# Polysketch attention and hash routing: attention written as a fixed pipeline over batches, with products of ones ahead of it and gather lists of the static slots alone

## The chip, the cores and the metric

The kernel runs on one core of one Trainium2 chip. The metric is the device time of one launch in microseconds (us); before the change it is 277.99 us, the median of three runs (277.56, 277.99 and 279.6). The engines are named as in the profile: PE (TensorE's matmuls) and PEld (its weight loads), DVE (VectorE), ACT (ScalarE), POOL (GpSimd), SP (SyncE, which here only issues DMAs).

## The reference

Attention with a polynomial feature map over 4 batches, 4 heads, 1088 positions and a head width of 32, then a mixture of 8 experts in which a token's id picks its expert:

```python
def phi(x):                                    # S1, S2: (8, 32), float64 in memory
    a = einsum('rd,bhsd->bhsr', S1, x); b = einsum('rd,bhsd->bhsr', S2, x)
    return einsum('bhsi,bhsj->bhsij', a, b).reshape(..., 64)
q_p, k_p = phi(q), phi(k)
num = q_p @ (k_p^T v);  den = q_p @ sum_s(k_p) + 1e-06
x = (num / den) as rows (4352, 128)            # one row per batch and position, heads side by side
e = token_ids * 2654435761 % 8
out[e == i] = relu(x[e == i] @ w1[i]) @ w2[i]  # w1: (8, 128, 1024), w2: (8, 1024, 128), float32
```

## The kernel before, in words

**Attention.** Of each batch's 1088 positions, 1024 are its main part (8 tiles of 128 positions) and 64 its tail. For the keys, `k_side` (lines 302 to 324) transposes two groups of 4 tiles on PE (`kT`, L309), copies them with ACT (L311), multiplies by the sketches (`ab`, L313), copies that with ACT (L316) and makes the 64 features on DVE (`kp`, L328). `kv_side` (lines 331 to 352) then sums the features times the values, with a column of ones for the denominator, over all tiles (`kv`, L340); ACT spreads the result over the matrix `m` in 16 copies (L349). `q_side` (lines 354 to 400) makes the features of the queries in two halves: blocks transposed on DVE (`qT`, L358), sketches on PE (`abq`, L365), features (`f`, L328) and transposes (`fT`, L378) on DVE. It multiplies them by `m` (`x`, L387), ACT copies (`xe`, L391), DVE inverts the denominators (`den`, L393 and L394), POOL divides (`xs`, L397), and ACT issues the store of the rows to the scratch tensor `x_rows` in HBM (L404). Written k0, q1 and so on below: the part with the number of the batch, from 0.

**The tails** of all four batches are features of one tile pair. Their keys are done first; their queries are done once, after batch 3's `kv` (line 412), from copies of `m` (`m_tail`, L351), and stored by four small DMAs (L415) ahead of batch 3's main rows.

**Routing.** Each expert has 2 x 288 static slots: the first 288 are filled from batches 0 to 2 alone, the others from all. A count by scans and three products (`cnt`, L191), then some forty small DVE operations (lines 188 to 258) give each token its slot. Lines 266 to 282 turn slots into lists: per 17 token columns, DVE compares (`row`, L270; `in_tile`, L273; two `til`, L277), and 34 PE products add up the token numbers (`idx_ps`, L280). The lists `get` and `put` have 68 columns: 36 tiles of static slots and 32 for tokens beyond them.

**Experts.** For 16 groups of 288 slots, POOL gathers rows by indirect DMA (`xg`, L424), PE transposes (`xp`, L464), multiplies by `w1` and `w2` (`hp`, L488; `op`, L496), transposes back (L475), and POOL scatters (L429). The first 18 tiles' gathers read only rows of batches 0 to 2. The loop behind it (line 517) serves tokens beyond the static slots; with these inputs no expert has more than 566 tokens, so it makes no turn.

**What sets the order.** Nothing is placed by hand: the framework's scheduler orders each engine's instructions, and DMAs wait for their buffers. Loads go out on SP (q, k, v, weights) and ACT (token ids and the 12 tail pieces, L88).

Of the kernel before, what the change touches and what calls it, by code (L numbers as in the profile page):

```python
# [9 lines left out]
F32 = mybir.dt.float32  # L10
# [14 lines left out]
def kernel(  # L25
# [12 lines left out]
    nc = tc.nc  # L38
# [38 lines left out]

    s64 = const.tile([2 * R, D, 2], I32)
# [29 lines left out]

    ident = const.tile([P, P], F32)
    make_identity(nc, ident[:])  # L110
    iota = const.tile([P, P], F32)
    nc.gpsimd.iota(iota[:], pattern=[[1, P]], base=0, channel_multiplier=0, allow_small_or_imprecise_dtypes=True)
    nval = const.tile([P, C], I32)
    nc.gpsimd.iota(nval[:], pattern=[[1, C]], base=1, channel_multiplier=C)
# [24 lines left out]
    ex = shifts("ex", hi, 1, 21)  # L139
    live = s_tile("live", F32)  # L140
    nc.vector.tensor_scalar(ex[:], ex[:], 127.0 - 1023.0, 0.0, op0=OP.add, op1=OP.max)
    nc.vector.tensor_scalar(ex[:], ex[:], 255.0, None, op0=OP.min)
    nc.vector.tensor_scalar(live[:], ex[:], 0.0, None, op0=OP.is_gt)
    nc.vector.tensor_scalar(ex[:], ex[:], 23, None, op0=OP.logical_shift_left)
    sg = s_tile("sg")
    nc.vector.tensor_scalar(sg[:], hi, 31, 31, op0=OP.logical_shift_right, op1=OP.logical_shift_left)
    nc.vector.tensor_tensor(sg[:], sg[:], ex[:], op=OP.bitwise_or)
    m_hi = shifts("m_hi", hi, 12, 9)
    m_lo = s_tile("m_lo")
    nc.vector.tensor_scalar(m_lo[:], lo, 29, None, op0=OP.logical_shift_right)  # L150
    top = s_tile("top")
    nc.vector.tensor_tensor(top[:], m_hi[:], m_lo[:], op=OP.bitwise_or)
    nc.vector.tensor_tensor(top[:], top[:], sg[:], op=OP.bitwise_or)
    rest = shifts("rest", lo, 3, 3)
    s32 = s_tile("s32", F32)
    nc.vector.tensor_copy(s32[:], rest[:])
    nc.vector.scalar_tensor_tensor(s32[:], s32[:], 2.0 ** -52, sg[:].bitcast(F32), op0=OP.mult, op1=OP.mult)
# [9 lines left out]
    s_k = const.tile([P, Q, 2, R], F32)  # L167
    nc.gpsimd.memset(s_k[:], 0.0)
    for t in range(Q):
# [7 lines left out]
    eid_i = const.tile([P, C], I32)  # L177
    nc.vector.tensor_scalar(eid_i[:], tok[:, :, 0], E - 1, None, op0=OP.bitwise_and)
    eid = const.tile([P, C], F32)
    nc.vector.tensor_copy(eid[:], eid_i[:])  # L180
    mask = hots.tile([P, E, C], F32)
    nc.vector.tensor_tensor(mask[:], eid[:].unsqueeze(1).to_broadcast([P, E, C]),
                            iota[:, 0:E].unsqueeze(2).to_broadcast([P, E, C]), op=OP.is_equal)
    seq = hots.tile([P, E, C], F32)
    nc.vector.tensor_tensor_scan(seq[:].rearrange("p e c -> p (e c)"), keep[:].rearrange("p e c -> p (e c)"),
                                 mask[:].rearrange("p e c -> p (e c)"), 0.0, op0=OP.mult, op1=OP.add)
    cp = const.tile([P, E], F32)
    nc.vector.tensor_copy(cp[:], seq[:, :, C - 1])
    cnt = bank([P, 3, E], "cnt")
    for n, w in enumerate((before, ones, early)):  # L190
        nc.tensor.matmul(cnt[:, n], w[:], cp[:], start=True, stop=True)  # L191
    first = const.tile([P, E], F32)
    nc.vector.tensor_copy(first[:], cnt[:, 0])

    took = const.tile([P, E], F32)
    nc.vector.tensor_scalar(took[:], cnt[:, 2], float(GN), None, op0=OP.min)
    nt_f = const.tile([P, E], F32)
    nc.vector.tensor_tensor(nt_f[:], cnt[:, 1], took[:], op=OP.subtract)
    nc.vector.tensor_scalar(nt_f[:], nt_f[:], float(P - 1 - GN), 0.0, op0=OP.add, op1=OP.max)
# [11 lines left out]
    past = hots.tile([P, OT, E], F32)  # L211
# [10 lines left out]
    def of_token(per_expert, name):  # L222

        both = hots.tile([P, E, C], F32, name=name + "_m")
        nc.vector.tensor_tensor(both[:], mask[:], per_expert[:].unsqueeze(2).to_broadcast([P, E, C]), op=OP.mult)
        t = const.tile([P, C], F32, name=name)
        nc.vector.tensor_reduce(t[:], both[:].rearrange("p e c -> p c e"), axis=AX.X, op=OP.add)
        return t

    nc.vector.tensor_tensor(seq[:], seq[:], first[:].unsqueeze(2).to_broadcast([P, E, C]), op=OP.add)  # L230
    nc.vector.tensor_mul(seq[:], seq[:], mask[:])
    rank = const.tile([P, C], F32)
    nc.vector.tensor_reduce(rank[:], seq[:].rearrange("p e c -> p c e"), axis=AX.X, op=OP.add)
    took_t = of_token(took, "took_t")
    jump_e = const.tile([P, E], F32)
    nc.vector.tensor_sub(jump_e[:], ends[:], nt[:])
    nc.vector.tensor_scalar(jump_e[:], jump_e[:], float(P), float((E - 1) * GN), op0=OP.mult, op1=OP.add)
    nc.vector.scalar_tensor_tensor(jump_e[:], iota[:, 0:E], float(-GN), jump_e[:], op0=OP.mult, op1=OP.add)
    jump = of_token(jump_e, "jump")
    pos = const.tile([P, C], F32)  # L240
    nc.vector.tensor_sub(pos[:], rank[:], took_t[:])
    nc.vector.scalar_tensor_tensor(jump[:], pos[:], float(GN), jump[:], op0=OP.is_gt, op1=OP.mult)

    late = const.tile([P, C], F32)
    nc.vector.memset(late[:], 1.0)
    nc.vector.tensor_scalar(late[0:EP], rank[0:EP], float(GN), None, op0=OP.is_gt)
    nc.vector.tensor_scalar(took_t[:], took_t[:], -1.0, float(E * GN), op0=OP.mult, op1=OP.add)
    nc.vector.tensor_add(took_t[:], took_t[:], jump[:])
    nc.vector.tensor_mul(took_t[:], took_t[:], late[:])
    nc.vector.tensor_add(rank[:], rank[:], took_t[:])  # L250
    nc.vector.scalar_tensor_tensor(rank[:], eid[:], float(GN), rank[:], op0=OP.mult, op1=OP.add)
    slot_i = const.tile([P, C], I32)
    nc.vector.tensor_scalar(slot_i[:], rank[:], -1.0, None, op0=OP.add)
    st_i = const.tile([P, 2, C], I32)
    nc.vector.tensor_scalar(st_i[:, 0], slot_i[:], P.bit_length() - 1, None, op0=OP.logical_shift_right)
    nc.vector.tensor_scalar(st_i[:, 1], slot_i[:], P - 1, None, op0=OP.bitwise_and)
    st = const.tile([P, 2, C], F32)
    nc.vector.tensor_copy(st[:], st_i[:])


    digit_i = const.tile([P, 2, C], I32)
    nc.vector.tensor_scalar(digit_i[:, 0], nval[:], 6, None, op0=OP.logical_shift_right)
    nc.vector.tensor_scalar(digit_i[:, 1], nval[:], 63, None, op0=OP.bitwise_and)
    digit = const.tile([P, 2, C], F32)
    nc.vector.tensor_copy(digit[:], digit_i[:])
    idx_ps = ps_x.tile([P, 2, NT], F32, tag="x", name="idx_ps")
    CH = C // 2
    for c0 in range(0, C, CH):
# [30 lines left out]
    for m in ms + m_tails:  # L299
        nc.gpsimd.memset(m[:], 0.0)  # L300
# [275 lines left out]
```

## Time and profile before

| | us |
|---|---|
| median of the runs shown | 277.99 |
| the profiled execution | 277.01 |
| its span, first to last instruction | 275.3 |
| PE busy in it | 224.0 |
| DVE busy | 103.5 |
| POOL busy | 96.0 |
| ACT busy | 69.8 |

The profile is of one execution, and 1.7 us of its time lie outside the span. The span has two halves: attention and routing, to about 118 us, in which engines wait for one another, and the experts, in which PE is busy almost without a gap. PE's records are modelled at their ends, so a run of like products is best read as its length divided by its count. The granted clock is a column of its own; 1.00 is 2.4 GHz and 0.50 is 1.2 GHz.

### The profile page before, as it was taken

The numbers are of one execution on the slowest core, as the hardware profiler recorded it, in microseconds if no ns is written. First come the engines' busy times: TensorE is split into PE (matmuls) and PEld (weight loads), VectorE is DVE, ScalarE is ACT, GpSimd is POOL, SyncE is SP. The second block draws the span as 40 slices with busy tenths as digits, with TensorE's granted clock in tenths as the row PEclk, the third lists the DMA queues.
The fourth block names the chain that finished last, engine by engine and source line by source line (L and its number), as shares of the span: only waits on it lengthen the run. The fifth ranks groups of instructions, "written<-read, shape, count | busy, mean of one in ns | idle before, by whom it ended". The sixth has DMA issues, their size and how long they took to land.

```text
span 275.3 us, 3183 instructions
## 1 busy us (share of the span) xinstructions
PE 224.0 (81%) x1109; PEld 188.0 (68%) x1110; DVE 103.5 (38%) x200; ACT 69.8 (25%) x197; POOL 96.0 (35%) x114
## 2 busy tenths in 40 slices
PE   0079898879896986427999999999999999999900
PEld 0069898869796986405777777777777777777600
DVE  6682992099614693001213213213223213222100
ACT  0121306112543233201322222332322332322200
POOL 7200003001640041277705565265562522421340
PEclk9999999988795695955999999999999999999975
DMA  5994344998110001031100111011110100000000
GB/s 164 275 340 124 87 144 120 337 343 268 78 79 0 0 2 76 19 114 49 48 12 24 43 38 41 30 36 35 47 39 19 45 21 18 17 18 15 19 26 8
DMA packets 22464, 22.14 MB, mean 80 GB/s; under 512 B 5178, under 2 KB 19771, under 8 KB 22448
## 3 DMA queue, kind: packets, MB, share of 16 engines
q1 hardware_dynamic: 15840, 14.69, 17.7%
q0 software_dynamic: 2304, 4.59, 5.8%
q10 hardware_dynamic: 4304, 2.66, 3.1%
q8 instruction: 9, 0.15, 0.2%
q14 instruction: 7, 0.06, 0.1%
HBM read 17.47 MB, written 4.59 MB: 80 GB/s over the span
## 4 chain that ended last, share of the span: by engine, by line
PE 59%; DMA 14%; issue 11%; ACT 6%; POOL 4%; DVE 3%; POOLq 1%; ACTq 0%; SPq 0%; DVEq 0%
PE hp L488 17%; PE op L496 14%; DMA out_dram<-os,put 9%; PE x_ps L387 7%; PE kv L340 6%; PE ab_ps L313 6%; ACT m L349 4%; PE abq_ps L365 3%; PE kT_ps L309 2%; POOL out_dram L429 2%; DMA k<-in_k_dram 2%; DMA q<-in_q_dram 2%; PE idx_ps L280 1%; ACT kT L311 1%; PE xp L464 1%
## 5 line engine op out<-in xcount | busy, mean ns | idle before, releaser
L488 PE MATMUL hp<-xT,w 128*128 128x288 f32 x256 | 84.8, 419 | 0.0
L496 PE MATMUL op<-hT,w 128*128 128x288 f32 x256 | 81.9, 406 | 0.0
L439 DVE TENSOR_SCALAR hT<-hp 128x288 f32<-128x288 f32 x64 | 29.3, 458 | 88.9 <-PE hp L488 88.9
L496 PEld LDWEIGHTS op<-hT,w 128*128 128x128 f32 x256 | 48.6, 190 | 13.3
L429 POOL DMA_INDIRECT out_dram<-os,put x36 | 35.8, 993 | 61.3 <-ACT os L437 30.4
L488 PEld LDWEIGHTS hp<-xT,w 128*128 128x128 f32 x256 | 48.3, 197 | 11.5
L437 ACT ACTIVATE hT<-hp 128x288 f32<-128x288 f32 x64 | 26.3, 411 | 67.1 <-PE hp L488 66.0
L424 POOL DMA_INDIRECT xg<-x_rows,get x36 | 36.5, 1015 | 17.4 <-PE xp L464 9.0
L387 PE MATMUL x_ps<-m,fT 128*128 128x132 f32 x128 | 24.4, 360 | 2.0 <-ACT m L349 1.4
L387 PEld LDWEIGHTS x_ps<-m,fT 128*128 128x128 f32 x128 | 22.5, 265 | 3.0 <-ACT m L349 2.1
L313 PE MATMUL ab_ps<-s_k,kT 128*128 128x64 f32 (+1 forms) x72 | 17.9, 422 | 6.1 <-ACT kT L311 6.1
L313 PEld LDWEIGHTS ab_ps<-s_k,kT 128*128 128x128 f32 (+1 forms) x72 | 16.3, 328 | 8.6 <-ACT kT L311 7.1
L397 POOL TENSOR_TENSOR xs<-xe,den 128x512 f32<-128x512 f32 (+1 forms) x9 | 11.5, 1296 | 30.4 <-DVE den L394 25.3
L319 POOL MEMSET va<- 128x32 f32 x4 | 0.6, 155 | 51.3 <-PE kv L340 51.3
L340 PE MATMUL kv<-va,kp 128*128 128x66 f32 x128 | 18.5, 309 | 0.0
L340 PEld LDWEIGHTS kv<-va,kp 128*128 128x128 f32 x128 | 18.2, 227 | 0.0
L349 ACT COPY m<-kv 32x66 f32<-32x66 f32 x64 | 13.2, 206 | 19.1 <-PE kv L340 18.2
L464 PE MATMUL xp<-ident,xg 128*128 128x128 f32 x36 | 7.6, 303 | 10.8 <-DMA xg<-x_rows,get 10.8
L464 PEld LDWEIGHTS xp<-ident,xg 128*128 128x128 f32 x36 | 5.0, 148 | 14.2 <-issue 8.0
L391 ACT COPY xe<-x_ps 128x396 f32<-128x396 f32 (+2 forms) x17 | 6.2, 380 | 26.8 <-PE x_ps L387 24.6
L365 PE MATMUL abq_ps<-s_k,qT 128*128 128x64 f32 (+1 forms) x72 | 12.7, 346 | 0.0
L365 PEld LDWEIGHTS abq_ps<-s_k,qT 128*128 128x128 f32 (+1 forms) x72 | 12.2, 262 | 0.4 <-issue 0.3
(129 smaller groups left out, 167.2 us busy)
## 6 DMA issues: line engine op xcount, KB each, us to landing
w<-in_moe_w_dram SPq DMA_DIRECT2D x16, 512.0 KB, 7.8
k<-in_k_dram SPq DMA_DIRECT2D x4, 512.0 KB, 4.6
v<-in_v_dram SPq DMA_DIRECT2D x4, 512.0 KB, 5.4
q<-in_q_dram SPq DMA_DIRECT2D x4, 512.0 KB, 5.2
x_rows<-xs ACTq DMA_DIRECT2D x4, 512.0 KB, 2.6
xg<-x_rows,get POOLq DMA_INDIRECT x36, 2.6
out_dram<-os,put POOLq DMA_INDIRECT x36, 2.3
k_tail<-in_k_dram ACTq DMA_DIRECT2D x4, 32.0 KB, 5.0
```

The costliest lines, as they stand in the source:

```text
L313: nc.tensor.matmul(ab_ps[:, g:g + w, h].rearrange("p t x r -> p t (x r)"), kT[:w * D, h], s_k[:w * D, 0:w].rearrange("p t x r -> p (t x r) ...
L340: nc.tensor.matmul(kv[:, pr], kp[rows, t, 2 * pr:2 * pr + 2].rearrange("p h i j -> p (h i j)"), va[rows, t, 2 * pr:2 * pr + 2].rearrange(" ...
L349: nc.scalar.copy(m[t * D:(t + 1) * D, h::2, f, t], src)
L365: nc.tensor.matmul(ab_ps[:w * D, g // Q, :, h].rearrange("p q x r -> p q (x r)"), qT[:, h, g:g + w].rearrange("p t s -> p (t s)"), s_k[:]. ...
L387: nc.tensor.matmul(p[rows, h], fT[r, (h0 + h) * FB + fb, rows], m[r, h0 + h, fb].rearrange("p t d -> p (t d)"), start=(fb == 0), stop=(fb ...
L424: nc.gpsimd.indirect_dma_start(out=dst[:], out_offset=None, in_=x_dram[0:rows], in_offset=bass.IndirectOffsetOnAxis(ap=idx, axis=0), bound ...
L429: st_ = nc.gpsimd.indirect_dma_start(out=out[:], out_offset=bass.IndirectOffsetOnAxis(ap=idx, axis=0), in_=src[:], in_offset=None, bounds_ ...
L437: nc.scalar.activation(dst, src, AF.Relu if relu else AF.Copy)
L439: nc.vector.tensor_scalar(dst, src, 0.0, None, op0=OP.max)
L464: nc.tensor.transpose(xp[:, i], xg[:], ident[:])
L488: nc.tensor.matmul(hp[:], w1[:, g % E, c * P:(c + 1) * P], columns(xTs, "xT", g * GN, (g + 1) * GN), start=True, stop=True)
L496: nc.tensor.matmul(ops[g][:], w2[:, g % E, c], hTs[g][:, c], start=(c == 0), stop=(c == FC - 1))
```

## The change

The attention is taken apart into steps and written in the order in which each engine is to issue them; `manual_schedule` holds all five engines to it up to `ordered.close()`. What comes behind that line is still placed by the scheduler.

- At the start PE makes 12 products of a tile of ones with 512 columns, and 2 more between the first transposes and the first sketches; their result is not used.
- All loads and the stores of the rows are issued by SP: batch 0, the 12 tail pieces, batches 1 to 3, experts 0 to 3; the rows of batch 0; experts 4 to 7; the other rows.
- Each batch's 64 tail queries are multiplied by `m` straight after its main ones (`x_tail_products`, 8 products of 33 columns), and stored with them. `m_tail` is gone.
- `m` of batch 3 is spread by ACT and DVE in turn (8 copies each).
- The lists have 36 columns. `row` is made in bf16, one token column at a time (34 operations); `in_tile` and the two `tiles` cover all columns at once. Tokens beyond the static slots find their numbers in the last loop, which makes no turn here.

```diff
+    def keep_busy(n):
+        p = ps_o.tile([P, 512], F32, tag="o", name="idle")
+        for _ in range(n):
+            nc.tensor.matmul(p[:], warm[:, 0:P], warm[:], start=True, stop=True)
+    keep_busy(WARM)
...
+    def route_rows(part):
+        for c in range(part * C // 2, (part + 1) * C // 2):
+            nc.vector.tensor_scalar(row1[:, c], iota_b[:], st[:, 1, c:c + 1], None, op0=OP.is_equal)
+    def route_tiles():
+        nc.vector.tensor_tensor(in_tile[:], iota[:, 0:ST].unsqueeze(1).to_broadcast([P, C, ST]),
+                                st[:, 0].unsqueeze(2).to_broadcast([P, C, ST]), op=OP.is_equal)
+        nc.vector.tensor_scalar(tiles[:, :, 0], in_tile[:], p1[:], None, op0=OP.mult)
+        nc.vector.tensor_tensor(tiles[:, :, 1], in_tile[:], iota[:, 0:C].unsqueeze(2).to_broadcast([P, C, ST]),
+                                op=OP.mult)
...
-                    nc.scalar.copy(m[t * D:(t + 1) * D, h::2, f, t], src)
+                    dst = m[t * D:(t + 1) * D, h::2, f, t]
+                    if b == B - 1 and t % 2:
+                        nc.vector.tensor_copy(dst, src)
+                    else:
+                        nc.scalar.copy(dst, src)
...
+    kTs = [transposed(k_t[0], g, Q) for g in range(0, T, Q)]
+    keep_busy(WARM2)
+    qT = q_blocks(q_t[0], T)
+    abk_ps = k_products(kTs, T)
+    abq_ps = q_products(qT, T)
...
+    cnt = route_counts()
+    abk = copied(abk_ps, lambda t: t[:])
+    abq = copied(abq_ps, lambda t: t[:])
+    kp = k_features(abk, T, work, "")
+    kTs = [transposed(k_tail, 0, TT)]
+    abt_ps = k_products(kTs, TT)
+    abt = copied(abt_ps, lambda t: t[:, :TT])
+    kTs = [transposed(k_t[1], g, Q) for g in range(0, T, Q)]
+    kp_tail = k_features(abt, TT, const, "_tail")
+    fTs = [q_features(abq, 0, slice(0, P), work, "", 2)]
+    qT_tail = q_blocks(q_tail, TT)
+    abt_ps = q_products(qT_tail, TT)
+    abt = copied(abt_ps, lambda t: t[:TT * D, 0:1])
+    fTs.append(q_features(abq, 1, slice(0, P), work, "", 2))
+    qT = q_blocks(q_t[1], T)
+    fT_tail = q_features(abt, 0, slice(0, TT * D), const, "_tail", 1)
     for b in range(B):
-        m = kv_side(b, tail)
-        if b < EB:
-            main_rows(b, m)
-    xs = q_side(q_tail, TT, [(slice(u * Q // 2, (u + 1) * Q // 2), m_tails[u]) for u in range(2)])
...
-    main_rows(B - 1, m)
+        kv = kv_products(b, (kp, va), (kp_tail, va_tail))
+        more = b + 1 < B
+        if more:
+            abk_ps = k_products(kTs, T)
+            abq_ps = q_products(qT, T)
+            va = values(v_t[b + 1], T, work, "")
+        if b == 0:
+            route_slots(cnt)
+        m = kv_diagonal(b, kv)
+        if more:
+            abk = copied(abk_ps, lambda t: t[:])
+            abq = copied(abq_ps, lambda t: t[:])
+            kp = k_features(abk, T, work, "")
+        x_products(fTs, m)
+        x_tail_products(b, m)
+        if b + 2 < B:
+            kTs = [transposed(k_t[b + 2], g, Q) for g in range(0, T, Q)]
+        if more:
+            fTs = [q_features(abq, 0, slice(0, P), work, "", 2)]
+        den = denominators()
+        x_rows(b, den)
+        if more:
+            fTs.append(q_features(abq, 1, slice(0, P), work, "", 2))
+        if b + 2 < B:
+            qT = q_blocks(q_t[b + 2], T)
+        if b == 0:
+            route_rows(0)
+            load_experts(range(E // 2, E))
+        if b == 1:
+            route_rows(1)
+            route_tiles()
+            route_end(route_list())
+    ordered.close()
```

Two places show what moves. The first is POOL at the end of attention, before the change: `xs` are the divisions (two of the tails' single one, then batch 3's), `xg` the gathers, `va` the values, `m_tail` the copies for the tails.

```order
L320 COPY va<-v_116 128x32x32
L351 COPY m_tail_327<-m_325 32x8x33
L397 TENSOR_TENSOR xs<-xe,den 128x4x4x32 x2
L351 COPY m_tail_328<-m_326 32x8x33
L397 TENSOR_TENSOR xs<-xe,den 128x4x2x32
L397 TENSOR_TENSOR xs<-xe,den 128x4x4x32 x2
L424 DMA xg<-x_rows,get 128x128 x15
```

The same place on POOL after the change (the first `xs` rows are batch 2's, the second batch 3's):

```order
L351 COPY va<-v_122 128x32x32
L439 TENSOR_TENSOR xs<-xe,den 128x4x4x32 x2
L445 TENSOR_TENSOR xs_tail<-xe,den 64x128
L545 DMA xg<-x_rows,get 128x128 x8
L439 TENSOR_TENSOR xs<-xe,den 128x4x4x32 x2
L445 TENSOR_TENSOR xs_tail<-xe,den 64x128
L545 DMA xg<-x_rows,get 128x128 x7
```

Before, every gather stood behind batch 3's divisions; now eight stand ahead of them, behind batch 2's.

The second place is DVE from batch 1's denominators on, after the change; `row`, `in_tile` and `tiles` are the last things that the 34 list products on PE need, and in PE's order these products stand between the transposes of batch 3's keys and the `kv` products of batch 2.

```order
L430 TENSOR_SCALAR den<-xe 128x36
L431 RECIPROCAL den<-den 128x36
L336 TENSOR_TENSOR f<-ab 128x1024
L403 STREAM_TRANSPOSE fT<-f 128x1024
L384 STREAM_TRANSPOSE qT<-q_120 128x1024
L272 TENSOR_SCALAR row_210<-iota_b,st 128x128 x17
L275 TENSOR_TENSOR in_tile<-iota,st 128x1224
L277 TENSOR_SCALAR tiles<-in_tile,p_155 128x34x36
L278 TENSOR_TENSOR tiles<-in_tile,iota 128x34x36
```

Before, the comparisons lay among batch 0's features and the list products between batch 2's key sketches and batch 0's `x`; now they come a batch later and behind batch 1's denominators.

## Rows read from the trace of the kernel before

**Rows 1.** The page: busy time of each engine, share of the span, instructions.
```profile
PE 224.0 (81%) x1109; PEld 188.0 (68%) x1110; DVE 103.5 (38%) x200; ACT 69.8 (25%) x197; POOL 96.0 (35%) x114
```
**Rows 2.** Stretches; columns: PE, PEld, DVE, ACT, POOL busy, granted clock, DMA share, GB/s.
```profile
10.00:20.00 10.00, 5.24 (x22) 4.31 (x22) 7.69 (x33) 2.54 (x4) 1.44 (x3) 1.00 1.08 324
...
30.00:40.00 10.00, 10.00 (x49) 10.00 (x49) 10.00 (x11) 0.59 (x1) 0.00 (x0) 1.00 0.53 159
...
85.00:93.00 8.00, 8.00 (x40) 7.55 (x41) 5.32 (x5) 0.70 (x2) 0.00 (x0) 0.50 0.00 0
94.50:102.00 7.50, 7.50 (x68) 7.36 (x67) 7.15 (x8) 1.68 (x6) 1.96 (x2) 1.00 0.01 2
...
113.30:118.00 4.70, 0.00 (x0) 0.00 (x0) 0.54 (x2) 0.66 (x2) 2.34 (x3) 1.00 0.09 23
118.60:127.00 8.40, 3.02 (x7) 1.34 (x7) 0.00 (x0) 0.90 (x2) 6.32 (x7) 0.50 0.31 99
```
**Rows 3.** Timeline of PE; columns: start, length, engine, line, operation, shapes, count.
```profile
33.44 3.63 PE L340 MATMUL kv<-va,kp 128*128 128x66 f32 x16
...
89.90 3.83 PE L387 MATMUL x_ps<-m,fT 128*128 128x132 f32 x16
...
95.80 2.02 PE L387 MATMUL x_ps<-m,fT 128*128 128x132 f32 x16
...
97.66 3.68 PE L340 MATMUL kv<-va,kp 128*128 128x66 f32 x32
...
107.57 5.68 PE L387 MATMUL x_ps<-m,fT 128*128 128x132 f32 x32
...
127.30 5.75 PE L488 MATMUL hp<-xT,w 128*128 128x288 f32 x14
```
**Rows 4.** Timeline of ACT, DVE and POOL; in brackets the idle time before.
```profile
5.76 0.16 DVE L136 TENSOR_SCALAR ex<-s 16x32 int32<-16x32 int32 x1
5.85 0.16 DVE L146 TENSOR_SCALAR sg<-s 16x32 int32<-16x32 int32 x1
...
68.53 3.53 ACT L349 COPY m<-kv 32x66 f32<-32x66 f32 x16 [2.77 <-PE kv L340]
68.70 3.44 DVE L328 TENSOR_TENSOR kp<-ab 128x1024 f32<-128x1024 f32 x2
69.04 4.01 POOL L397 TENSOR_TENSOR xs<-xe,den 128x512 f32<-128x512 f32 x2
...
94.71 2.36 DVE L328 TENSOR_TENSOR kp<-ab 128x1024 f32<-128x1024 f32 x2 [2.41 <-ACT ab L316]
...
115.49 2.05 POOL L397 TENSOR_TENSOR xs<-xe,den 128x512 f32<-128x512 f32 x2 [5.11 <-ACT xe L391]
...
117.71 1.23 POOL L424 DMA_INDIRECT xg<-x_rows,get  x1 [0.17 <-issue]
```
**Rows 5.** Groups by line and shape; columns: busy us, mean ns of one, idle before.
```profile
L328 DVE TENSOR_TENSOR f<-abq 128x1024 f32<-128x1024 f32 x8 | 10.1, 1256 | 1.9 <-ACT abq L371 1.9
L378 DVE STREAM_TRANSPOSE fT<-f 128x1024 f32<-128x1024 f32 x8 | 9.9, 1242 | 0.2
L309 PE MATMUL kT_ps<-ident,k 128*128 128x128 f32 x32 | 8.1, 404 | 0.0
...
L277 DVE TENSOR_TENSOR til<-in_tile,digit 128x1156 bf16<-128x1156 f32 x4 | 5.2, 1345 | 0.0
...
L270 DVE TENSOR_TENSOR row<-iota,st 128x2176 bf16<-128x2176 f32 x2 | 4.8, 2422 | 11.9 <-PE idx_ps L280 11.9
...
L311 ACT COPY kT<-kT_ps 128x512 f32<-128x512 f32 x8 | 4.7, 587 | 12.9 <-PE kT_ps L309 12.9
...
L280 PE MATMUL idx_ps<-til,row 128*128 128x136 bf16 x34 | 3.9, 301 | 1.3 <-DVE til L277 1.3
```
**Rows 6.** The chain that ended last, in order of time: its first piece.
```profile
1.61 4.62 DMA k<-in_k_dram
```
**Rows 7.** The page's DMA issues: KB each, median us from issue to landing.
```profile
x_rows<-xs ACTq DMA_DIRECT2D x4, 512.0 KB, 2.6
```

More of the change, by code (lines that the diff above doesn't have):

```diff
@@ L184 @@
[L184 to L192, printed above, removed]
@@ L193 @@
-    nc.vector.tensor_copy(first[:], cnt[:, 0])
-    took = const.tile([P, E], F32)
[L196 to L199, printed above, removed]
+    took = const.tile([P, E], F32)
+    left = const.tile([P, E], F32)
+    pos = const.tile([P, C], F32)
+    st = const.tile([P, 2, C], F32)
@@ new lines, with route_counts @@
+    row1 = hots.tile([P, C, P], BF16)
+    tiles = hots.tile([P, C, 2, ST], BF16)
+    in_tile = hots.tile([P, C, ST], BF16)
+    put = const.tile([P, ST], I32)
+    get = const.tile([P, ST], I32)
+    def route_counts():
+        eid_i = const.tile([P, C], I32, name="eid_i")
+        nc.vector.tensor_scalar(eid_i[:], tok[:, :, 0], E - 1, None, op0=OP.bitwise_and)
+        nc.vector.tensor_copy(eid[:], eid_i[:])
+        nc.vector.tensor_tensor(mask[:], eid[:].unsqueeze(1).to_broadcast([P, E, C]),
+                                iota[:, 0:E].unsqueeze(2).to_broadcast([P, E, C]), op=OP.is_equal)
+        nc.vector.tensor_tensor_scan(seq[:].rearrange("p e c -> p (e c)"), keep[:].rearrange("p e c -> p (e c)"),
+                                     mask[:].rearrange("p e c -> p (e c)"), 0.0, op0=OP.mult, op1=OP.add)
+        cp = const.tile([P, E], F32, name="cp")
+        nc.vector.tensor_copy(cp[:], seq[:, :, C - 1])
+        cnt = bank([P, 3, E], "cnt")
+        for n, w in enumerate((before, ones, early)):
+            nc.tensor.matmul(cnt[:, n], w[:], cp[:], start=True, stop=True)
+        return cnt
@@ new lines, in transposed, with k_products @@
+    def transposed(src, g, w):
+        p = bank([P, H, P], "kT_ps")
+        for h in range(H):
+            nc.tensor.transpose(p[:w * D, h], src[:, h, g:g + w].rearrange("p t d -> p (t d)"), ident[:])
+        kT = work.tile([P, H, P], F32, tag="kT", name="kT")
+        nc.scalar.copy(kT[:w * D], p[:w * D])
+        return kT
+    def k_products(kTs, n):
+        ab_ps = bank([P, T, H, 2, R], "ab_ps")
+        for g, kT in zip(range(0, n, Q), kTs):
+            w = min(Q, n - g)
+            for h in range(H):
+                nc.tensor.matmul(ab_ps[:, g:g + w, h].rearrange("p t x r -> p t (x r)"), kT[:w * D, h],
+                                 s_k[:w * D, 0:w].rearrange("p t x r -> p (t x r)"), start=True, stop=True)
+        return ab_ps
@@ new lines, in q_blocks, with q_products @@
+    def q_blocks(src, n):
+        qT = work.tile([P, H, n, D], F32, tag=f"qT{n}", name="qT", bufs=1)
+        nc.vector.transpose(qT[:].rearrange("p h t s -> p (h t s)"), src[:].rearrange("p h t d -> p (h t d)"))
+        return qT
+    def q_products(qT, n):
+        ab_ps = bank([P, GQ, Q, H, 2, R], "abq_ps")
+        for g in range(0, n, Q):
+            w = min(Q, n - g)
+            for h in range(H):
+                nc.tensor.matmul(ab_ps[:w * D, g // Q, :, h].rearrange("p q x r -> p q (x r)"),
+                                 qT[:, h, g:g + w].rearrange("p t s -> p (t s)"),
+                                 s_k[:].rearrange("p q x r -> p (q x r)"), start=True, stop=True)
+        return ab_ps
@@ new lines, in x_tail_products @@
+    def x_tail_products(b, m):
+        u, t = b % 2, b // 2
+        rows, r = slice(u * SP, (u + 1) * SP), slice(t * D, (t + 1) * D)
+        p = ps_x.tile([P, H, DA], F32, tag="x", name="x_ps")
+        for h in range(H):
+            for fb in range(FB):
+                nc.tensor.matmul(p[rows, h], fT_tail[r, h * FB + fb, rows], m[r, h, fb, t],
+                                 start=(fb == 0), stop=(fb == FB - 1), skip_group_check=True,
+                                 tile_position=(r.start, rows.start))
+        nc.scalar.copy(xe[rows, GQ * H * Q:], p[rows])
@@ L231 @@
[L231 to L256, printed above, removed]
```

386 lines of the change are left out of this document (205 added, 181 removed).

## The prediction

> **What bounds the kernel now.** The busy line of the page comes first: PE 224.0 us of 275.3, the other engines below 104 [rows 1]. That is an average over two halves, so the table of stretches and the timelines come next. In the experts' half PE is hardly idle and the change doesn't touch it. The numbers to hold on to are two: its first long run of `hp` products begins at 127.30 [rows 3], and from there to the end of the span are 275.3 - 127.3 = 148.0 us. So the question is when this run can begin.
>
> In the attention half no engine is full. Between 113.3 and 118.0 PE does nothing, from 118.6 to 127.0 it works 3.02 us of 8.40 [rows 2]: batch 3's last `x` products are done, and the chain of divisions, store, gather and transposes runs with nothing beside it. The first gather starts at 117.71 behind batch 3's divisions [rows 4], 9.6 us ahead of the `hp` run; two `hp` records, some 0.9 us, are done before that run.
>
> PE's clock has two levels there. `x` costs 3.83 us for 16 records at 89.90 and 2.02 at 95.80; `kv` 3.63 for 16 at 33.44 (0.227 each) and 3.68 for 32 at 97.66 (0.115) [rows 3]. The granted clock reads 0.50 and 1.00 around the later ones. Around the early `kv` it reads 1.00 too, although the lengths are those of the low level; I go by the lengths, since no change of level is on record before. PE was busy 10.00 us of 10 at 30 to 40 and stayed low [rows 2]; the level rose inside runs of `x`: 32 records at 107.57 take 5.68 us, where 32 would be 7.7 low and 4.0 high [rows 3]. It fell after PE had stood still: 1.00 during the idle stretch from 113.3, 0.50 in the one after it [rows 2].
>
> **The change, part by part.** I follow the chain in the new order, in us from the span's start.
>
> *Start.* The products of ones stand before `k0`. A 512-column product isn't in the trace; the list products (3.9 us busy for 34, 136 columns) bound it: 0.115 each if the columns cost nothing, 0.43 if all the time is columns [rows 5]. Twelve are 1.4 to 5.2 us; I take 4.3. `k0`, issued at 1.61, lands at 6.2 [rows 6], as I expect it to again, so they hide behind that load; what I take them to do is to lift the clock early. Then: `k0` transposes 1.1 (8 of 32 that took 8.1; half that at the high level), two ACT copies of 0.59 [rows 5], and handovers, to 8.8; key sketches (16 records at `kv`'s rate, their width being nearly the same) 2.0, to 10.8; query sketches 2.0, three counts 0.8, the tail's transposes 0.5, copy 0.6, sketches 1.0, copy 0.3, with handovers 16.2. DVE is then the last: tail key features 0.7, `f` and `fT` 1.26 + 1.24 [rows 5], the tail queries' block transpose 0.45: 19.8. Four sketches of the tail queries on PE follow, 1.1, and `kv0` starts at 21.0; it started at 33.44 [rows 3]. At the low level it would be 24.5. The tail loads now stand on SP between batch 0 and batch 1; `k1` is needed at 16 and its issue slips to about 12, so it lands about when it is wanted; the 3.5 us between 21.0 and 24.5 cover a little lateness too.
>
> *Batches 0 and 1.* By 21 PE has waited some 2 us for DVE, so I take its clock as low again. `kv0` has 36 records at 0.227: to 29.1. Sketches of batch 1, 32 records: 7.6, to 36.7. DVE does the second half of batch 0's queries, `q1`'s transpose, the tail's features and the slots (35 small operations at the mean of 7.69 / 33 = 0.23 of a like stretch [rows 2], 8.0) until 34.0, then `kp1`. ACT spreads `m` in 3.5 [rows 4] beside the sketches. `x0` lifts the clock: half its records low, half high, 5.6, to 42.3; tail products 1.1 and `k2` transposes 1.1, to 44.5. Batch 1 at the high level: `kv1` 4.2, sketches 4.0, `x1` 4.0, tail and transposes 2.2, to 58.9.
>
> *The list products.* PE's order puts them here, ahead of `kv2`, and DVE has them ready only after denominators (from 58.3, 0.55), half of batch 2's features (2.5, and 0.5 for sharing with POOL), `q3`'s transpose 1.25, 17 `row` comparisons, `in_tile` and two `tiles`. `til` over 1156 elements took 1.35, so `in_tile` and the second `tiles` over 1224 are 1.43 each; the first, which has only one tensor to read, is 0.3 to 1.4, taken 0.9. A `row` operation over 128 columns is bounded below by 0.09, the step between two of 32 columns [rows 4], and above by 0.2 (2.42 for 17 columns is 0.142 each, as one instruction [rows 5], and 0.06 for a start of its own); 0.12 is taken, 2.0 for 17. Sum: 69.0. So PE stands still from 58.9 to 69.0, a new wait of 10.1 us, and the clock falls. Removed are two `row`, two `in_tile`, four `til`, 13 us of DVE. The bounds of the new ones are -1.1 and +1.9.
>
> The Trainium skill (VectorE: DVE Perf Modes, on the trn2 errata) says that each operation from SBUF pays a fixed latency, so that many small tiles pay it many times; this speaks against 34 `row` operations in place of two. By its table one would be 0.094 if four elements go per cycle and 0.194 at one, and the sum below 262.6 or 264.3; no row here shows which.
>
> *Batches 2 and 3.* List products 4.2 (3.9 busy as now, and the handover), to 73.2. `kv2` and its sketches low, 8.1 + 7.5, to 88.8; `x2` rises midway, 5.6, tail 1.1, to 95.5; `kv3` high, to 99.7. Batch 2's rows meanwhile: denominators 0.55, divisions 2.05 [rows 4] and 0.35 for the tail's, sharing 0.5: 99.5; two issues of 0.35, 2.6 to landing [rows 7]: the first gather at 102.8. Eight gathers now stand ahead of batch 3's divisions. `m3` is handed from ACT to DVE and back 16 times, 0.22 of a copy and 0.05 each, 4.3 against 3.5; `x3` starts on its first quarters and, low again after that wait, ends with its tail at 109.3, inside the gathers' time. So `hp` starts at 102.8 + 9.6 = 112.4, a gather's path as now. Batch 3's rows are needed by the 19th tile only, and are stored by 120.
>
> *Sum.* 112.4 + 148.0 + 0.9 = 261.3 of span, and 1.7 outside it: 263.0, against 277.0 of the profiled execution. The median of the runs shown is 1.0 higher, so measured values may be too. Nearly all of the gain of 14 is the path from batch 3 to the experts: `kv3` ends only 2 us earlier than now (97.66 + 3.68 + 0.6 = 101.9), though `kv0` starts 12 earlier; the wait for the lists eats the rest.
>
> **The rivals.** *Clock high (25%).* If the clock rises in the list products or `kv2`, then `kv2`, the sketches and `x2` are 3.5 + 3.6 + 1.6 us shorter, and the result is 254. For it: the list products are dense, and the products of ones may have this very purpose. Against: 10 us of busy PE at 30 to 40 left it low [rows 2]. The Trainium skill (TensorE: Matmul & The Clock Gate, Part 1) has the clock released by sustained matmul activity; by that `kv2` would do it, and the early `kv` of this trace contradicts it.
>
> *DVE and POOL in each other's way (12%).* The `kp` pair took 3.44 beside divisions of 4.01, and 2.36 alone, as the divisions took 2.05 alone [rows 4]. If the chain before the list products is stretched likewise, 10.6 x 0.46 = 4.9, and the divisions of batch 2 by 2.0, the result is 270.
>
> *The early gathers aren't early (6%).* If the first of them waits for all stores, as now, it starts behind 109.3 + 0.4 + 0.55 + 2.9 + 3.3 = 116.5 and the result is 277: no change. Against: its rows are those of batches 0 to 2, and it stands ahead of the last divisions.
>
> *The clock never rises in attention (7%), slower.* `x` is now four groups of 8 records, each freed by an ACT copy; if these breaks keep the level low, `x0` ends at 44, `x1` at 70, the list products at 87 (DVE is behind `x1` as before), `x2` at 109, `kv3` at 119, `x3` with its tail at 131.5. PE, not the gather, is then last: `hp` at 132, 132 + 148.9 + 1.7 = 282.6. It decides from about `x3` ending at 125. Against: each rise now came within such products.
>
> **How the numbers follow.** The forecast as summed, 263, own range 257 to 268, has 50%. Below it lies the high clock, above it DVE with POOL; 251 to 272 leaves out about a fifth. Faster by over 1% (below 275.2; 1% is about what runs of this kernel, 277.56 to 279.6, can tell): forecast, clock and DVE, 86%. Within 1%: 7%. Slower: 7%.
>
> **What would show it.** Right: `kv0` near 21; PE idle before the list products with DVE as releaser, 8 to 12 us; eight gathers before batch 3's divisions; the `hp` run near 112. Wrong: `kv2` at 0.115 per record (clock), a gather behind batch 3's store, or `x0` at 0.24 throughout.

## The result and the profile after

The changed kernel takes 258.17 us (median of 4 runs, 257.17 to 259.19) against 278.34 (277.56 to 279.6) of the kernel before beside it: ratio 0.927, 95% interval 0.922 to 0.932. The profiled execution took 257.97, of which 256.3 are the span. The prediction was 263.0, range 251 to 272. In some experiments below, runs of one kernel lie 6 to 12 us apart; where a profile shows why, PE's clock fell or held behind a wait, so ranges are given beside the medians.

The page of the changed kernel first: busy times, the shares of the chain that ended last, batch rows' DMA issues.

```profile
PE 223.1 (87%) x1155; PEld 186.0 (73%) x1156; DVE 99.2 (39%) x232; ACT 69.1 (27%) x192; POOL 95.8 (37%) x114
...
PE 76%; DVE 6%; issue 5%; DMA 4%; POOL 3%; ACT 1%; POOLq 1%; DVEq 0%; ACTq 0%
...
x_rows<-xs SPq DMA_DIRECT2D x4, 512.0 KB, 2.8
```

PE works as long as before [rows 1]; what went is time in which it stood, 275.3 - 224.0 = 51.3 us then and 256.3 - 223.1 = 33.2 now. Its timeline (columns as in [rows 3], in brackets the idle time before):

```profile
6.83 1.34 PE L314 MATMUL kT_ps<-ident,k 128*128 128x128 f32 x8
...
20.77 7.09 PE L361 MATMUL kv<-va,kp 128*128 128x66 f32 x32
...
35.72 4.99 PE L412 MATMUL x_ps<-m,fT 128*128 128x132 f32 x32
...
42.62 3.69 PE L361 MATMUL kv<-va,kp 128*128 128x66 f32 x32
...
66.02 2.22 PE L284 MATMUL idx_ps<-tiles,row 128*128 128x72 bf16 x34 [9.69 <-DVE tiles L278]
68.05 7.07 PE L361 MATMUL kv<-va,kp 128*128 128x66 f32 x32
...
82.98 5.25 PE L412 MATMUL x_ps<-m,fT 128*128 128x132 f32 x32
...
89.20 3.79 PE L361 MATMUL kv<-va,kp 128*128 128x66 f32 x32
...
97.61 5.79 PE L412 MATMUL x_ps<-m,fT 128*128 128x132 f32 x26 [0.20 <-DVE m L376]
...
106.50 5.68 PE L609 MATMUL hp<-xT,w 128*128 128x288 f32 x16
```

The long `hp` run starts at 106.50; before it was 127.30 [rows 3]. The new wait of 9.69 stands where the prediction put it, and `kv` takes 7.07 for 32 records behind it, 3.79 a batch later. The stretches (columns as in [rows 2]) show in turn batch 1 with the end of batch 0, mostly at the high clock (0.94 in the mean), the wait (0.62), and the work behind it at the low clock (0.50):

```profile
35.70:56.30 20.60, 20.60 (x182) 19.92 (x181) 15.12 (x30) 9.92 (x32) 4.29 (x5) 0.94 0.97 302
56.30:66.00 9.70, 0.03 (x1) 0.00 (x0) 9.52 (x24) 0.76 (x2) 3.15 (x3) 0.62 0.69 217
66.00:83.00 17.00, 16.98 (x103) 16.74 (x103) 3.30 (x8) 3.89 (x17) 1.19 (x2) 0.50 0.00 0
```

DVE's end of the lists, and POOL's divisions and gathers, which answer to [rows 4]:

```profile
46.23 3.62 DVE L272 TENSOR_SCALAR row<-iota_b,st 128x128 bf16<-128x128 bf16 x17
...
59.89 2.82 DVE L272 TENSOR_SCALAR row<-iota_b,st 128x128 bf16<-128x128 bf16 x17
62.62 1.43 DVE L275 TENSOR_TENSOR in_tile<-iota,st 128x1224 bf16<-128x1224 f32 x1
64.08 0.54 DVE L277 TENSOR_SCALAR tiles<-in_tile,p 128x1224 bf16<-128x1224 bf16 x1
64.54 1.43 DVE L278 TENSOR_TENSOR tiles<-in_tile,iota 128x1224 bf16<-128x1224 bf16 x1
...
90.42 2.85 POOL L439 TENSOR_TENSOR xs<-xe,den 128x512 f32<-128x512 f32 x2 [13.92 <-ACT xe L426]
...
96.93 1.23 POOL L545 DMA_INDIRECT xg<-x_rows,get  x1 [3.31 <-DMA x_rows<-xs_tail]
...
107.30 2.05 POOL L439 TENSOR_TENSOR xs<-xe,den 128x512 f32<-128x512 f32 x2
```

The first gather waits for batch 2's store alone and runs at 96.93, while PE works on batch 3's `x`; batch 3's divisions come behind eight gathers, at 107.30.

### The profile page after: what moved, and what is told of

It reads as the page before. It is cut to its first block, busy times and chain, and to the rows that moved or that the text cites. A ratio compares the mean times of both kernels' runs of the same rounds, so it can differ in the third digit from the quotient of the medians.

```text
span 256.3 us, 3312 instructions
## 1 busy us (share of the span) xinstructions
PE 223.1 (87%) x1155; PEld 186.0 (73%) x1156; DVE 99.2 (39%) x232; ACT 69.1 (27%) x192; POOL 95.8 (37%) x114
## 4 chain that ended last, share of the span: by engine, by line
PE 76%; DVE 6%; issue 5%; DMA 4%; POOL 3%; ACT 1%; POOLq 1%; DVEq 0%; ACTq 0%
PE op L617 24%; PE hp L609 23%; PE kv L361 8%; PE ab_ps L325 5%; PE abq_ps L393 4%; PE x_ps L412 4%; PE idle L152 2%; DMA xg<-x_rows,get 2%; PE tp L596 2%; POOL xg L545 2%; DMA out_dram<-os,put 1%; DVE f L336 1%; PE xp L585 1%; PE kT_ps L314 1%; DVE row L272 1%
## 5 line engine op out<-in xcount | busy, mean ns | idle before, releaser
L439 POOL TENSOR_TENSOR xs<-xe,den 128x512 f32<-128x512 f32 x8 | 10.5, 1331 | 36.9 <-ACT xe L426 13.9
L412 PE MATMUL x_ps<-m,fT 128*128 128x132 f32 x128 | 21.6, 339 | 2.3 <-DVE m L376 2.3
L361 PE MATMUL kv<-va,kp 128*128 128x66 f32 x128 | 21.6, 349 | 0.0
L361 PEld LDWEIGHTS kv<-va,kp 128*128 128x128 f32 x128 | 21.1, 262 | 0.2
L336 DVE TENSOR_TENSOR kp<-ab 128x1024 f32<-128x1024 f32 x8 | 9.6, 1248 | 13.4 <-ACT ab L331 13.4
L325 PE MATMUL ab_ps<-s_k,kT 128*128 128x64 f32 (+1 forms) x72 | 13.1, 354 | 0.7 <-ACT kT L316 0.7
L325 PEld LDWEIGHTS ab_ps<-s_k,kT 128*128 128x128 f32 (+1 forms) x72 | 12.3, 265 | 1.6 <-ACT kT L316 1.0
L403 DVE STREAM_TRANSPOSE fT<-f 128x1024 f32<-128x1024 f32 (+1 forms) x9 | 11.2, 1244 | 3.0 <-PE x_ps L412 2.5
L619 ACT COPY oT<-op 128x288 f32<-128x288 f32 x16 | 6.4, 399 | 19.4 <-PE op L617 19.4
L336 DVE TENSOR_TENSOR f<-ab 128x1024 f32<-128x1024 f32 (+1 forms) x9 | 10.7, 1192 | 2.1 <-ACT ab L331 2.1
```

Source lines behind the costliest of these rows:

```text
L325: nc.tensor.matmul(ab_ps[:, g:g + w, h].rearrange("p t x r -> p t (x r)"), kT[:w * D, h], s_k[:w * D, 0:w].rearrange("p t x r -> p (t x r) ...
L336: nc.vector.tensor_tensor(dst, ab[:, :, 0].unsqueeze(3).to_broadcast(shape), ab[:, :, 1].unsqueeze(2).to_broadcast(shape), op=OP.mult)
L361: nc.tensor.matmul(kv[:, pr], kp[rows, t, 2 * pr:2 * pr + 2].rearrange("p h i j -> p (h i j)"), va[rows, t, 2 * pr:2 * pr + 2].rearrange(" ...
L412: nc.tensor.matmul(p[:, h], fT[:, (h0 + h) * FB + fb], m[:, h0 + h, fb].rearrange("p t d -> p (t d)"), start=(fb == 0), stop=(fb == FB - 1 ...
```

## The experiments

The theory: most of the gain is the early gathers; the place of the list products costs PE the wait and then a low clock; the products of ones pay by the clock at the start. The rivals stand with each run, and times are set against the changed kernel's 258.17 us. The kernel before, run beside each group, had medians of 277.42 to 278.34 us, so differences of about 1 us between groups tell nothing.

**1. No products of ones.**

```diff
-    keep_busy(WARM)
-    keep_busy(WARM2)
```

> The products of ones are left out, both the 12 and the 2. Theory (they buy a high clock for the first transposes and sketches, which stand on the chain to kv of batch 0): the 8 transposes, 16 key sketches and 16 query sketches cost about 2.0, 3.6 and 3.6 us in place of 1.1, 2.0 and 2.0, so that kv of batch 0 starts at about 24 in place of 20.8, and the time is about 261.5, 3 to 4 us more than the 258.2 of the changed kernel. Rival (DVE sets the start of kv anyway, or the level rises in the first sketches by itself): kv starts within 0.7 us of 20.8 and the time is 257.5 to 259.

261.37 us (260.36 to 262.86), 3.2 above the changed kernel. Timeline of PE:

```profile
5.73 1.97 PE L313 MATMUL kT_ps<-ident,k 128*128 128x128 f32 x8
7.57 3.65 PE L324 MATMUL ab_ps<-s_k,kT 128*128 128x64 f32 x16
11.01 3.62 PE L392 MATMUL abq_ps<-s_k,qT 128*128 128x64 f32 x16
...
24.32 7.09 PE L360 MATMUL kv<-va,kp 128*128 128x66 f32 x32
```

The transposes start 1.1 us earlier than in the changed kernel's profile (6.83), where the 12 ones took 5.30. In the profiles of runs 2, 3 and 7 the ones took 4.19 to 4.44 and the transposes start at 5.86 to 5.91, so there they are all but hidden. Without the ones, the transposes and sketches are at the low level, and `kv` starts 3.55 later, as the theory has it.

**2. No early gathers.**

```diff
-                gather(xg, ..., NE if done_in + i < HT else N)
+                gather(xg, ..., N)
```

> Every gather is told that it may read all rows of x_rows, so that the first ones too wait for batch 3's store; nothing else differs. Theory (the first 18 tiles' gathers, which wait for batch 2's store alone, are what lets the experts begin while batch 3 is worked on): batch 3's divisions start about 105, and the first gather 5.7 to 6.5 us behind that, at about 111 in place of 96.9; the long hp run starts about 9.6 behind it, at 120.5 in place of 106.5, and the time is about 271 (268 to 273). Rival (PE's order alone made the kernel faster, and the experts wait for the last x products anyway): hp starts by 109 and the time is under 261.

The four runs are 262.93, 263.72, 270.43 and 271.4; their median, 267.07, is neither the theory's time nor the rival's. The profile is of the first; in it the clock rises midway through `kv` of batch 2, as it did not in the changed kernel, though PE has the same instructions up to there:

```profile
67.74 4.44 PE L361 MATMUL kv<-va,kp 128*128 128x66 f32 x32
```

The two slower runs have no profile, but their mean granted clock is on record: 0.845 and 0.846, against 0.868 and 0.862 in the faster two. So the level of the clock, some 8 us here, hides what the gathers are worth; runs 4 and 5 hold it high.

**3. The list products behind batch 2's `x`.**

```diff
         if b == 1:
             route_rows(1)
             route_tiles()
+        if b == 2:
             route_end(route_list())
```

> The 34 list products and the few DVE operations that read them are moved from ahead of kv of batch 2 to behind batch 2's tail products; DVE makes row, in_tile and tiles where it did. Theory (the wait of 9.7 us and the low clock behind it are both the price of where the list products stand): kv of batch 2 starts at about 56.5 in place of 68.1 and stays at 0.115 each, x of batch 2 ends near 69 in place of 88, kv of batch 3 runs from about 72, the hp run starts at 87 to 89 in place of 106.5, and the time is about 240 (237 to 244). Rival (the wait is only exchanged: DVE with its list work, the divisions or the loads hold batch 2 or 3 up instead): hp does not start before 98 and the time is over 249.

239.41 us (233.93 to 240.38): 18.8 less. Timeline of PE and POOL:

```profile
55.68 3.69 PE L361 MATMUL kv<-va,kp 128*128 128x66 f32 x32
...
68.30 1.28 PE L284 MATMUL idx_ps<-tiles,row 128*128 128x72 bf16 x34
...
78.39 1.23 POOL L546 DMA_INDIRECT xg<-x_rows,get  x1 [3.57 <-DVE m L376]
...
87.97 4.05 PE L610 MATMUL hp<-xT,w 128*128 128x288 f32 x16
```

No wait of that length takes the place of the one removed; PE's longest from there to the `hp` run is 2.15, for `m` of batch 3. This is what the theory expected.

**4. Ones in the wait.**

```diff
+            keep_busy(40)
             route_end(route_list())
```

> Forty more products of ones with 512 columns stand on PE ahead of the list products, so that PE works through the wait for DVE; nothing else differs. Theory (standing still is what drops the clock, and the clock is about half of the wait's price): at the high level the forty take about 8.8 us, list products start at about 66 as before, kv of batch 2 takes about 0.115 each in place of 0.22, its x products end near 80 in place of 88, and the time is about 250 (248 to 252). Rival (the level falls in kv and sketches whatever stands ahead of them): kv of batch 2 stays at 0.22 and the time is 257 to 260, or near 266 if the forty run at the low level too.

249.07 us (248.2 to 249.15), 9.1 less. PE:

```profile
56.87 8.58 PE L152 MATMUL idle<-warm 128*128 128x512 bf16 x39
66.49 1.28 PE L284 MATMUL idx_ps<-tiles,row 128*128 128x72 bf16 x34 [1.04 <-DVE tiles L278]
67.61 3.76 PE L361 MATMUL kv<-va,kp 128*128 128x66 f32 x32
```

The lists are no earlier, but `kv` takes 3.76 in place of 7.07. So of the 18.8 us that the place of the list products costs, 9.1 are the clock; the 9.7 that are left agree with the wait of 9.69.

**5. Ones in the wait, no early gathers** (the edits of 2 and 4).

> The forty products of ones in the wait of PE, as in the run that had them alone (249.07 us), and every gather waiting for batch 3's store. With the ones the level of the clock in batch 2 should be the same in all runs, so that this pair shows the gathers alone. Theory (the early gathers are worth a path from batch 3's divisions to the experts, less what the last x products take of it): first gather at about 103 in place of 88, hp run at about 112.5 in place of 97.8, time 262.5 (260 to 264.5), and no run near 270. Rival (the two times of the earlier run without early gathers, 263 and 271, have another cause than the clock in batch 2): the runs again lie some 8 us apart.

262.82 us (260.71 to 263.17). Against run 4, the early gathers are worth 262.82 - 249.07 = 13.75 us, and no run is near 270. The first gather is at 88.14 in run 4 (upper line) and at 102.58, behind batch 3's store, in run 5:

```profile
88.14 1.23 POOL L546 DMA_INDIRECT xg<-x_rows,get  x1 [3.33 <-DMA x_rows<-xs_tail]
...
102.58 1.23 POOL L546 DMA_INDIRECT xg<-x_rows,get  x1 [3.63 <-DMA x_rows<-xs_tail]
```

Run 5 makes the gathers later than they were in the kernel before. There the first stood behind batch 3's divisions, by its place in POOL's order, and started 0.17 after them [rows 4]; here it waits 3.63 for the store too. Some 3.5 of the 13.75 us are therefore no gain of the change, which leaves about 10 (an estimate from these two waits; no run has the gathers late by their place alone).

**6. The list products as in 3, and ones where PE waits for the second batch's keys.**

```diff
+    keep_busy(11)
     kTs = [transposed(k_t[1], g, Q) for g in range(0, T, Q)]
```

> The list products behind batch 2's x (239.4 us), and 11 more products of ones where PE waits for the second batch's keys at about 14 to 16.5. Theory (this wait is what drops the clock for kv of batch 0, the sketches behind it and half of x, some 8 us of PE; DVE is busy 13.7 of 14.9 us there and gives back a part): kv of batch 0 takes about 3.7 in place of 7.1, kv of batch 1 waits for DVE's kp and starts at about 34.5 in place of 42.1, and the time is about 234 (232.5 to 235.5), which would also be the cause of the one run of 233.93 among those of 239 to 240. Rival (DVE bounds batches 0 and 1 altogether): 238 to 240. Second rival (the level falls in kv of batch 0 anyway): kv stays at 7.1, time 239 to 241.

233.71 us (231.92 to 234.98). PE:

```profile
19.03 3.79 PE L361 MATMUL kv<-va,kp 128*128 128x66 f32 x32
...
39.47 3.17 PE L393 MATMUL abq_ps<-s_k,qT 128*128 128x64 f32 x16 [0.60 <-DVE qT L384]
42.43 6.00 PE L412 MATMUL x_ps<-m,fT 128*128 128x132 f32 x32
```

`kv` of batch 0 is at the high level. A part of the gain is given back on DVE, where the theory put it, but in another way: PE waits 0.60 for DVE's transpose, and behind that wait the clock falls (1.00 from 39 to 40, 0.52 from 40 to 42). That 233.93 in run 3 was an execution with `kv` of batch 0 high fits its mean granted clock, 0.940 against 0.911 and 0.912 in the other three (0.931 to 0.947 here); no profile shows it.

**7. Batch 2's denominators first, lists behind `kv` of batch 3, `m` of batch 3 by ACT alone.**

```diff
+            if b == 2:
+                den = denominators()
             fTs = [q_features(abq, 0, slice(0, P), work, "", 2)]
...
-                    if b == B - 1 and t % 2:
-                        nc.vector.tensor_copy(dst, src)
...
+        if b == 3:
+            route_end(route_list())
```

> The list products behind kv of batch 3, where PE waits for m; m of batch 3 spread by ACT alone; and batch 2's two denominator operations on DVE ahead of the features of batch 3's queries. Theory (in the run with the lists behind x of batch 2, the chain that sets the hp run was batch 2's denominators, which stood 2.3 us behind features on DVE, then divisions, store and six gathers): the denominators come at 68.7 in place of 70.9, the first gather at about 76 in place of 78.4, hp at 85.6 in place of 88.0, and the time is about 237 (235.5 to 238). Rival (batch 3's m and x set hp): with m by ACT alone x of batch 3 ends at about 81.5 in place of 85, but the time would then also be about 236, with the gathers' rows idle behind PE; what tells them apart is whether PE waits for a gather ahead of hp (theory) or not (rival).

238.75 us (237.82 to 241.15), a miss: no gain that can be told from run 3. The first gather came at 76.96, and PE waited for gathers, as theory said; but now only five stand ahead of batch 3's divisions on POOL, and PE stops inside the `hp` run for the sixth:

```profile
85.11 1.62 PE L610 MATMUL hp<-xT,w 128*128 128x288 f32 x6
89.41 0.33 PE L586 MATMUL xp<-ident,xg 128*128 128x128 f32 x1 [2.67 <-DMA xg<-x_rows,get]
```

**8. `row` by one comparison of two tensors for each half.**

```diff
-        for c in range(part * C // 2, (part + 1) * C // 2):
-            nc.vector.tensor_scalar(row1[:, c], iota_b[:], st[:, 1, c:c + 1], None, op0=OP.is_equal)
+        r = slice(part * C // 2, (part + 1) * C // 2)
+        nc.vector.tensor_tensor(row1[:, r], iota[:].unsqueeze(1).to_broadcast([P, C // 2, P]),
+                                st[:, 1, r].unsqueeze(2).to_broadcast([P, C // 2, P]), op=OP.is_equal)
```

> Each half of row is made by one comparison of two tensors over 17 columns, as in the kernel before, in place of 17 operations with a number per partition. Theory (an operation of 128 columns pays a start of its own, so the 17 are no cheaper together than one large one): one takes about 2.42 as before, against 2.82 for the 17 of the second half and 3.62 of the first; PE's wait ahead of the list products is 9.3 in place of 9.7, and the time lies within 1 us of 257.8. Rival (the small operations go faster per column): the large one takes over 3 us.

One run, 249.72, where within 1 us of 257.8 was expected. The rows are as expected (2.38, and 3.18 for the first half), but `kv` of batch 0 stayed high, with nothing in its path changed:

```profile
19.78 4.00 PE L362 MATMUL kv<-va,kp 128*128 128x66 f32 x32
...
51.56 2.38 DVE L272 TENSOR_TENSOR row<-iota,st 128x2176 bf16<-128x2176 f32 x1
...
57.26 2.22 PE L285 MATMUL idx_ps<-tiles,row 128*128 128x72 bf16 x34 [9.75 <-DVE tiles L279]
```

**9. The changed kernel with only the 11 ones of run 6.**

> The changed kernel with 11 more products of ones ahead of the transposes of the second batch's keys, and nothing else; the list products stand where the change put them. Theory (the wait of 1 to 3 us for those keys drops the clock, and kv of batch 0 with what follows costs 8 us for it; the single run of 249.72 with the rows made whole owed its gain to a clock that happened to stay high there, not to the rows): kv of batch 0 takes about 3.8 in place of 7.1, list products start near 57.5 in place of 66, the time is about 250 (248.5 to 251.5). Rival (the rows made whole were worth that much): kv of batch 0 may be shorter, but the time stays at 256 or above.

251.75 us, the runs 243.59, 250.53, 252.96 and 255.49. The median is just above the 248.5 to 251.5 expected, and the spread was not expected. The profile is of the run of 250.53:

```profile
19.39 3.79 PE L361 MATMUL kv<-va,kp 128*128 128x66 f32 x32
...
57.42 2.22 PE L284 MATMUL idx_ps<-tiles,row 128*128 128x72 bf16 x34 [10.54 <-DVE tiles L278]
59.44 7.07 PE L361 MATMUL kv<-va,kp 128*128 128x66 f32 x32
```

`kv` of batch 0 is high and the list products come at 57.42, with the rows as they were. So the 8 us of run 8 need no better rows. Why the four runs lie 12 us apart isn't shown by one profile; two waits from which the clock may or may not fall would do it. The run of 243.59 has the highest mean granted clock, 0.926, but the other three (0.881 to 0.893) do not sort by theirs.

**10. Run 6 with batch 3's divisions on DVE** (`nc.vector` for `nc.gpsimd` where b is 3).

> The list products behind batch 2's x and the 11 products of ones at the second batch's keys (233.7 us), with batch 3's divisions on DVE in place of POOL, so that nothing stands between the gathers on POOL. Theory (in that run POOL's divisions held the ninth gather up by 2.9 us, and PE waited 2.6 us ahead of its second run of hp for it): gathers follow each other every 1.3 us, the second run of hp starts at about 86.7 in place of 89.1, time about 231.3 (230 to 232.5). Rival (the gathers' own pace of 1.3 us a tile is the limit, so the wait only comes later): 233 to 234.5.

232.4 us (231.79 to 232.99). The gathers follow each other every 1.3 us and PE doesn't wait for the ninth, but the first `hp` run is at the low level (4.05 in run 6), so 1.7 of the 2.6 are given back:

```profile
82.05 5.74 PE L612 MATMUL hp<-xT,w 128*128 128x288 f32 x16
```

The ranges of the two kernels overlap, and the two profiles differ ahead of the divisions too (`kv` of batch 0 starts at 22.11 here and at 19.03 in run 6), so a gain from this edit alone isn't shown.

**11. Run 10 with the edits of run 7.**

> As the run with batch 3's divisions on DVE, and with batch 2's denominators ahead of the features on DVE, the list products behind kv of batch 3, and m of batch 3 by ACT alone. Theory (the chain from batch 2's denominators to the first gathers sets the first hp run; by the run that had these three alone the first gather comes 1.4 us earlier, and what it gained there was given back when only five gathers stood ahead of batch 3's divisions on POOL, which now stand on DVE): about 230 (228.5 to 231.3), 1 to 2 us under the run without them. Rival (the end is set by PE in the experts' half once hp has begun, with gathers behind it): no difference from that run, within 0.5 us.

229.8 us (229.16 to 229.97), ratio to the kernel before 0.825, interval 0.820 to 0.830: the fastest here, 28 us under the changed kernel. The first gather is at 70.41 (72.65 in run 10) and `hp` begins 2.3 earlier:

```profile
70.41 1.23 POOL L548 DMA_INDIRECT xg<-x_rows,get  x1 [2.83 <-PE x_ps L409]
...
79.74 1.33 PE L612 MATMUL hp<-xT,w 128*128 128x288 f32 x2 [0.37 <-ACT xT L561]
```

No run takes the hand-made order itself, the loads on SP or the narrower lists out of the changed kernel; what each of these is worth is not shown.

## Why the prediction was right, and where its terms were off

The time came out 4.8 us under the forecast, by the forecast's own mechanism, though one share of the gain was put too high. In the profiled execution, step by step (predicted, measured, and the difference that had gathered by then):

| step | predicted | measured | gathered |
|---|---|---|---|
| `kv0` starts | 21.0 | 20.77 | -0.2 |
| `kv1` starts | 44.5 | 42.62 | -1.9 |
| `k3` transposes end | 58.9 | 56.3 | -2.6 |
| list products start | 69.0 | 66.02 | -3.0 |
| `kv2` starts | 73.2 | 68.05 | -5.1 |
| `kv3` starts | 95.5 | 89.20 | -6.3 |
| first gather | 102.8 | 96.93 | -5.9 |
| `hp` run | 112.4 | 106.50 | -5.9 |
| `hp` run to the end | 148.9 | 149.8 | -5.0 |

- *The list products* are the largest mis-sized term: 4.2 against 2.0. The price was taken over from 136 columns [rows 5]; with 72 columns 34 took 2.22 at the low level, 1.28 at the high. A row of another width needs a bound for the columns too.
- *Start.* The 12 ones took 5.30 here, beyond their bound of 5.2, and held the first transposes up by 1.1; in other profiles they took as little as 4.15 (run 9). "Hidden" was nearly right, and the clock paid back more: without them `kv0` starts 3.55 later (run 1).
- *Batch 0* was 1.7 shorter than forecast, mostly by two terms: sketches 6.9 (28.84 to 35.72) against 7.6, and `x` rose earlier, 4.99 against 5.6.
- *DVE's chain*: the wait is right, 9.69 against 10.1, in part by luck. The 17 `row` operations took 2.82 where 2.0 was taken (0.166 each); the first `tiles`, 0.54 where 0.9 was taken, and the features, 2.5 without the 0.5 for sharing, made up for it. The 0.3 at the low end for `tiles` and the 0.06 for the start of a `row` operation have no row behind them; the measured values lie within both ranges. In the first half a `row` is 0.213 in the mean, because one of the 17 took 1.06 beside POOL's copy of `va` (1.04). Run 8 shows what 17 cost over one large one: 2.82 against 2.38, and 3.62 against 3.18. By the Trainium skill (VectorE: DVE Perf Modes, the trn2 errata) each operation pays a fixed latency. These pairs go that way, by 0.44 us in 17, but the two forms differ in operation and input type too, so they don't measure it. The measured 0.166 lies between the 0.094 and 0.194 that the prediction worked out from that table.
- *The clock.* Low in `kv0` and behind the wait, high in batch 1 and `kv3`: all as forecast. The rival with the high clock (25%) came true in none of the four runs of the changed kernel, and yet can come down to the execution: run 2's profile, with the same instructions on PE up to there, shows `kv2` rise. The reason against it, that PE busy with `kv` stays low, holds for the changed kernel (16.98 us of 17.00 at 0.50) and not for every run. The Trainium skill (TensorE: Matmul & The Clock Gate, Part 1) has sustained matmul activity release the clock; by these two traces it may or may not do so in `kv2`.
- *"Nearly all of the gain is the path from batch 3 to the experts"* is too much, and here the forecast's time came out better than its account. `kv3` was to end 2 us earlier than before. The last records of `kv3`, before (upper line) and after, put it 8.3 earlier:

```profile
101.27 0.66 PE L340 MATMUL kv<-va_tail,kp_tail 64*128 64x66 f32 x4
...
92.92 0.66 PE L361 MATMUL kv<-va_tail,kp_tail 64*128 64x66 f32 x4
```

  The `hp` run moved by 127.30 - 106.50 = 20.8, so the path behind `kv3` gave 12.5, about three fifths. Run 5 against 4 gives 13.75 for the gathers, of which some 10 are the change's.
- *"The wait for the lists eats the rest"* counts 10 as the wait. The place of the list products costs 18.8 (run 3), since the low clock behind the wait comes on top; the rival with the high clock priced that at 8.7, and run 4 gives 9.1.
- *Batch 2's rows.* The terms named add up to 95.5 + 3.45 = 98.95 and not to 99.5; the handover from the last `x` product to the denominators, which isn't named, measured 0.41 (89.27 to 89.68).
- *m of batch 3* handed to and fro: `x3`'s long run starts 4.0 after `kv3`'s end, as forecast (4.3), and no gain over ACT's 3.5.
- *DVE and POOL in each other's way*: only 0.8, in batch 2's divisions (2.85 against 2.05). The other two rivals fell: the gathers were early and the clock rose in `x0`. The rival with late gathers said that they wait for all stores "as now"; that was a misreading, for the first gather of the kernel before started 0.17 behind the divisions [rows 4], too soon for a store that takes 2.6 to land [rows 7].

## What to carry to other kernels

When an order is fixed by hand, look at each place where an in-order engine can stand: an instruction that needs a long chain elsewhere belongs behind work that is ready, even if its own result is wanted soon. A stop of TensorE cost twice here, as the wait (9.7 us) and as the slow products behind it (9.1 us), and filling the wait with products of ones gave back the second part. And look what each DMA really waits for: the gathers of rows of the first three batches needed nothing of the fourth, but stood behind its divisions in POOL's order. Ahead of them they were worth some 10 us here, and 13.75 against waiting for its store as well.

## What was not expected of the hardware

The clock also fell while PE did not stand at all. In run 5 PE was busy throughout from 66 to 84 (stretches of it):

```profile
80.00:82.00 2.00, 2.00 (x20) 2.00 (x20) 1.88 (x4) 0.03 (x1) 1.02 (x1) 1.00 0.00 0
82.00:84.00 2.00, 2.00 (x12) 2.00 (x12) 1.25 (x1) 0.00 (x0) 2.00 (x3) 0.53 0.00 0
```

The granted clock is 1.00 in the first two us and 0.53 in the next two, all of them `kv` of batch 3. Nothing here says why. And equal instruction streams gave either level (`kv2` in 7.07 or 4.44, `kv0` in 7.09 or 4.00). The wait ahead doesn't sort them: PE waited 2.06 for the second batch's keys in run 8, where `kv0` rose, and 1.07 in the changed kernel and 3.06 in run 2, where it stayed low. So a kernel with such waits has several times, 8 us apart: a single run of it can show a gain that its edit doesn't have, as run 8 did.
